# Splitting x earlier, halving the norm's maximum and lower parts, and one weight split per token tile

## The chip, the cores and the metric

The kernel runs on one core of one Trainium2 chip. The metric is the device time of one execution in microseconds. A core has TensorE (PE, matrix products into PSUM banks; PEld is its weight load), VectorE (DVE), ScalarE (ACT), GpSimd (POOL) and SyncE (SP, which issues the DMAs). Each engine works through its own row of instructions in order. An instruction whose operand isn't ready holds everything behind it in the row.

## The reference

Attention over 2 x 12 heads of 448 tokens with 64 columns, then two feed-forward networks on the 896 tokens, all in fp32:

```python
scores = cap * np.tanh(scale * (q @ k.T) / cap)
x = softmax(scores) @ v                 # heads side by side: 896 x 768
h = x @ w_in                            # 896 x 1024
e = np.exp(h - h.max(-1))
solu = h * e / (e.sum(-1) + 1e-9)
ln = (solu - solu.mean(-1)) / np.sqrt(solu.var(-1) + 1e-6) * g_ln
y = ln @ w_out                          # 896 x 768
p = sigmoid(y @ w_gate) * (y @ w_val)   # 896 x 1536
out = p @ moe2_w_out                    # 896 x 768
```

## The kernel before, in words

**Products in three passes.** An fp32 operand is split into an upper part, rounded to the multiplier's format (a cast on ACT), and a lower part, the rest (a subtraction on DVE or POOL). A product is then three matrix instructions: upper x upper, upper x lower, lower x upper. The weights arrive as 64-bit words and are turned to fp32 by bit operations on DVE (lines 320 to 323) before they are split.

**Stages.** Attention runs first, by pairs of heads. Two of the seven token tiles of the first network (128 tokens each, t = 0 and 1) are worked beside it, in slots of a table (`at`, `phase`). Tile 2 is begun at its end. The loop at line 584 does t = 2 to 6: first the 36 products of layer 1 for tile t (`l1_mms`, line 390), then `ln_trans(t - 1)`, eight transposes of the tile before, then the norm's chain of tile t. Layer 2 follows (line 620, the rows that write l2o and big from lnhi and lnlo): tokens 0 to 383 first, for each kk = 0 to 7 of the inner dimension six products (two rounds of kk = 0 to 3, then kk = 4 to 7 with all six), and after kk = 4 the transposes of tile 6. Then come tokens 384 to 895, then layer 3 (the gates) and layer 4.

**The norm's chain of a tile.** `ln_max` is a DVE maximum over the 1024 columns in PSUM (line 400). `ln_exp` is an exponential with its sum on ACT (405), into a tile e of which there is one. `ln_he` multiplies h and e on DVE (408). `ln_stats` takes two halves of statistics, their aggregate and a sum on DVE (415 to 419), and an inverse root on POOL (420). `ln_norm` takes a bias on DVE (424) and the scaled e on ACT (426, `late`). After the transposes, `ln_evac` casts the tile on ACT (440) and takes the lower part on DVE (441).

**What lies between.** `x_split(t)` makes the parts xh and xl of x that tile t's products read (377 and 378). There are two buffers of each, so tile t + 2 takes those of tile t. `w2_split(kk)` makes the two parts of w_out's slab kk, w_hi on ACT (515) and w_lo on DVE (512). They wait in the list `todo`, from which `fill(2)` takes the next slab's two steps. Before each kk, layer 2 calls `fill(1)` until that slab is there (lines 644 and 649).

**What sets the order.** Up to the end of layer 2, PE, ACT, DVE and POOL run in the order in which the code is written (`manual_schedule`, line 444). The weights of layer 3 (`load_slabs`, line 665: L315 and L337 on ACT, L320 to L323 and L340 on DVE) stand outside that order and are placed between by the scheduler. Two banks l2o serve layer 2; a later product takes a bank once the parts of y are taken from it (629 and 630).

Of the kernel before, what the change touches and what calls it, by code (L numbers as in the profile page):

```python
# [10 lines left out]
F32 = mybir.dt.float32  # L11
# [4 lines left out]
ALU = mybir.AluOpType  # L16
AX = mybir.AxisListType
# [3 lines left out]
P = 128  # L21
# [14 lines left out]
GROUPS = ((0, G1), (G1, NT))  # L36
# [11 lines left out]
L1_BESIDE = 2  # L48
# [20 lines left out]
def f32(ap):  # L69
    return ap.bitcast(F32)  # L70
# [7 lines left out]
def fused_kernel(ctx: ExitStack, tc: tile.TileContext, qk, v, cap, w_in, w_mid, g_ln, w_gv, w_fin, outT):  # L78
# [52 lines left out]
    with tc.If(bounded > 0) as cmp:  # L131
        network(tc, sh, False, w_in, w_mid, w_gv, w_fin, outT)
# [5 lines left out]
def network(ctx: ExitStack, tc: tile.TileContext, sh, general, w_in, w_mid, w_gv, w_fin, outT):  # L138
    nc = tc.nc
# [18 lines left out]
    lin2 = wi.enter_context(tc.tile_pool(name="lin2" + sfx, bufs=2, side="left"))  # L158
# [129 lines left out]
    def fill(k):  # L288
        for _ in range(min(k, len(todo))):
            todo.popleft()()  # L290
# [76 lines left out]
    hts, sts, lnes = {}, {}, {}  # L367

    def x_split(t, eng=nc.vector):
        xh = lin2.tile([P, K1, P], F32R, tag="xh", name="xh")  # L370
        xl = lin2.tile([P, K1, P], F32R, tag="xl", name="xl")
        t0 = t * P
        for b in range(B):
            lo, hi_ = max(t0, b * S), min(t0 + P, (b + 1) * S)
            if lo < hi_:
                src = x_sb[b][:, :, lo - b * S:hi_ - b * S]
                nc.scalar.copy(xh[:, :, lo - t0:hi_ - t0], src)  # L377
                eng.tensor_tensor(xl[:, :, lo - t0:hi_ - t0], src, f32(xh[:, :, lo - t0:hi_ - t0]), ALU.subtract)  # L378
        x_parts[t] = xh, xl

    def l1_mms(t):

        out = []

        def mm(half, kk, m):
            if t not in hts:
                hts[t] = big()
            xh, xl = x_parts[t]
            l, r = ((xh, wi_hi), (xh, wi_lo), (xl, wi_hi))[m]
            nc.tensor.matmul(hts[t][:, half], l[:, kk], r[:, half, kk], start=(kk == 0 and m == 0), stop=(kk == K1 - 1 and m == 2))  # L390

        for half in range(2):
            for kk in range(K1):
                for m in range(3):
                    out.append(lambda half=half, kk=kk, m=m: mm(half, kk, m))
        return out

    def ln_max(t):
        sts[t] = lin2.tile([P, 24], F32, tag="st", name="st")
        nc.vector.tensor_reduce(sts[t][:, 0:1], hts[t].rearrange("p a b -> p (a b)"), AX.X, ALU.max, negate=True)  # L400

    def ln_exp(t):
        st = sts[t]
        lnes[t] = lin2.tile([P, F1], F32, tag="e", name="e", bufs=1)
        nc.scalar.activation(lnes[t], hts[t].rearrange("p a b -> p (a b)"), AF.Exp, bias=st[:, 0:1], accum_out=st[:, 1:2])  # L405

    def ln_he(t):
        nc.vector.tensor_tensor(lnes[t], hts.pop(t).rearrange("p a b -> p (a b)"), lnes[t], ALU.mult)  # L408
# [21 lines left out]
    def ln_trans(t):  # L430
        e = lnes[t]
        lnes[t] = tp = big()
        for kk in range(K2):
            nc.tensor.transpose(tp[:, kk // 4, (kk % 4) * P:(kk % 4 + 1) * P], e[:, kk * P:(kk + 1) * P], ident)

    def ln_evac(t):
        g = 0 if t < 3 else 1
        c = slice(t * P - GROUPS[g][0], t * P - GROUPS[g][0] + P)
        tv = lnes.pop(t).rearrange("p a (k b) -> p (a k) b", b=P)
        nc.scalar.copy(ln_hi[g][:, :, c], tv)  # L440
        nc.vector.tensor_tensor(ln_lo[g][:, :, c], tv, f32(ln_hi[g][:, :, c]), ALU.subtract)  # L441


    order = nullcontext() if general else tc.manual_schedule(engines=ORDERED)
# [20 lines left out]
    def at(slot, phase, f, *a):  # L465
        beside.setdefault((slot, phase), []).append(lambda: f(*a))

    def run(fs):
        while fs:
            fs.pop(0)()  # L470
# [5 lines left out]
    for t in range(L1_BESIDE):  # L476
        s0 = S_L1 + L1_SLOTS * t
        s1 = s0 + L1_SLOTS
        at(s0, 2, x_split, t)
        for k in range(L1_SLOTS):  # L480
            at(s0 + 1 + k, 0 if k else 2, lambda t=t, k=k: run(l1_mms(t)[n_mm * k:n_mm * k + n_mm]))
        at(s1, 3, ln_max, t)
        at(s1 + 1, 1, ln_exp, t)
        at(s1 + 1, 2, ln_he, t)
        at(s1 + 1, 2, ln_stats, t)
        at(s1 + 1, 3, ln_norm, t)
        at(s1 + 3, 0, ln_trans, t)
        at(s1 + 3, 1, ln_evac, t)
        if t == L1_BESIDE - 1:
            at(s1, 2, x_split, t + 1)  # L490

# [15 lines left out]
    def w2_split(kk):  # L507
        g, w, hi = sh.g_sb[:, kk:kk + 1], f32(w2_w[kk]), w2_hi[:, kk]

        def lower():  # L510
            lo = w2a.tile([P, DM], F32R, tag="w", name="w2_lo")
            nc.vector.scalar_tensor_tensor(lo, w, g, f32(hi), ALU.mult, ALU.subtract)  # L512
            w2.append((hi, lo))

        return [lambda: nc.scalar.activation(hi, w, AF.Identity, scale=g), lower]
# [49 lines left out]
    t = L1_BESIDE  # L565
# [5 lines left out]
    late = []  # L571
# [12 lines left out]
    for t in range(L1_BESIDE, 7):  # L584
        if t == 2:
            x0.close()
            lnt2 = lns.enter_context(tc.tile_pool(name="lnt2" + sfx, bufs=1, side="right", reuse_waits="tile"))
            ln_hi[1] = lnt2.tile([P, K2, NT - G1], F32R, name="lnhi1")
            ln_lo[1] = lnt2.tile([P, K2, NT - G1], F32R, name="lnlo1")
            w2b = lns.enter_context(tc.tile_pool(name="w2b" + sfx, bufs=1, side="right", reuse_waits="tile"))  # L590
            w2_hi = w2b.tile([P, K2, DM], F32R, name="w2_hi")
            for kk in range(K2):
                todo.extend(w2_split(kk))
        mms = mms[24:] if t == L1_BESIDE else l1_mms(t)
        run(mms)
        if t > L1_BESIDE:
            ln_trans(t - 1)
        else:
            run(late[:1])
        ln_max(t)  # L600
        fill(2)
        ln_exp(t)
        ln_he(t)
        ln_stats(t)
        if t > L1_BESIDE:
            ln_evac(t - 1)
        else:
            run(late[1:])
        ln_norm(t, True)
        if t + 2 < 7:  # L610
            x_split(t + 2, nc.gpsimd)
            fill(2)
    wi.close()
    ytp = ctx.enter_context(tc.tile_pool(name="ytp" + sfx, bufs=1, side="left", reuse_waits="tile"))
    y_hi = ytp.tile([P, K3, NT], F32R, name="y_hi")
# [7 lines left out]
    def l2_mm(o, m, g, kk):  # L623
        w = [part[:, m * P:(m + 1) * P] for part in w2[kk]]
        prods(o, w, ln_hi[g][:, kk], ln_lo[g][:, kk], kk == 0, kk == K2 - 1)
# [14 lines left out]
    for ms in ((0, 1, 2, 3), (4, 5)):  # L640
        b = big()
# [6 lines left out]
    for kk in range(W2_EARLY, K2):  # L648
        while len(w2) <= kk:
            fill(1)  # L650
        for m in range(K3):
            l2_mm(accs[m], m, 0, kk)
        if kk == W2_EARLY:
            ln_trans(6)
            ln_evac(6)
    for m in range(K3):
        y_evac(accs[m], m, 0)
    for m in range(K3):
# [35 lines left out]
    for fc in range(K4):  # L694
# [4 lines left out]
        for z in range(2):  # L699
            o = big()  # L700
            for hf in range(2):
                for kk in range(K3):
                    c = slice(hf * HT, hf * HT + HT)
# [11 lines left out]
    for m in range(DM // P):  # L715
# [3 lines left out]
        for hf in range(2):  # L719
            c = slice(hf * HT, hf * HT + HT)  # L720
# [41 lines left out]
```

## Time and profile before

| | |
|---|---|
| median of 3 runs | 517.36 us (516.28 to 517.64) |
| profiled execution | 517.01 us, of which the span is 515.2 us |
| PE busy | 496.3 us, 96% of the span |
| DVE, ACT, POOL busy | 307.8, 235.6, 57.0 us |
| granted clock of TensorE | 1.00 |

The span runs from the profile's first instruction to its last. A busy PE is a modelled figure: its instructions are pipelined, so the start of one to the start of the next tells what it costs, and its duration is longer than that. A wait is written as the idle time before an instruction, with what ended it.

### The profile page before, as it was taken

What the parts mean: (1) busy time and instruction counts of PE and PEld (TensorE: products, weight loads), DVE (VectorE), ACT (ScalarE), POOL (GpSimd) and SP (SyncE); (2) the same over time, 40 slices, a digit from 0 to 9 for tenths busy, and PEclk for the clock granted to TensorE, in tenths of its full rate; (3) what the DMA queues carried; (4) which work ended last, traced back from release to release, by engine and by line L of the source; (5) the groups of instructions that cost most, each with busy time, mean ns of one, the idle gap of its engine ahead of it and who ended that gap; (6) DMA issues with size and microseconds to landing.
All of it is one profiled execution on the core that took longest, in us unless ns stands there. A gap on an engine that the chain in (4) does not pass through costs nothing.

```text
span 515.2 us, 6254 instructions
## 1 busy us (share of the span) xinstructions
PE 496.3 (96%) x2496; PEld 385.6 (75%) x2496; DVE 307.8 (60%) x416; ACT 235.6 (46%) x288; POOL 57.0 (11%) x41
## 2 busy tenths in 40 slices
PE   8999999998988889999999999999999999999995
PEld 5323323544566669988899999999999999999995
DVE  0778787556576686721488767767766675553000
ACT  4999999675325552410354333433233322232100
POOL 0010220103021210000010111111111011000000
PEclk9999999999999999999999999999999999999999
DMA  7757568633000003120045433333333323400001
GB/s 256 232 184 247 180 190 273 195 98 124 36 1 1 1 0 122 28 98 0 1 132 185 153 95 110 123 102 93 113 123 122 116 80 131 158 37 36 20 36 41
DMA packets 15313, 55.03 MB, mean 107 GB/s; under 512 B 2796, under 2 KB 5740, under 8 KB 15276
## 3 DMA queue, kind: packets, MB, share of 16 engines
q1 hardware_dynamic: 15276, 54.56, 33.2%
q8 instruction: 21, 0.34, 0.3%
q14 instruction: 16, 0.13, 0.1%
HBM read 51.68 MB, written 2.79 MB: 106 GB/s over the span
## 4 chain that ended last, share of the span: by engine, by line
PE 82%; ACT 8%; DVE 7%; issue 1%; POOL 1%; DMA 0%; ACTq 0%; POOLq 0%
PE big L620 37%; PE l4o L620 17%; PE l2o L620 8%; PE o L228 7%; PE big L188 6%; PE big L390 3%; PE sums L231 3%; ACT e L194 2%; ACT e L216 2%; DVE e L408 1%; DVE st L400 1%; DVE w_lo L512 1%; ACT e L405 1%; ACT e L426 1%; DVE lnlo L441 1%
## 5 line engine op out<-in xcount | busy, mean ns | idle before, releaser
L620 PE MATMUL big<-y_hi,w_hl 128*128 128x448 f32 x576 | 161.6, 362 | 0.0
L620 PEld LDWEIGHTS big<-y_hi,w_hl 128*128 128x128 f32 x576 | 107.9, 187 | 8.0
L620 PE MATMUL big<-y_lo,w_hl 128*128 128x448 f32 x288 | 104.6, 363 | 0.0
L620 PE MATMUL l4o<-p_hi,w_hl 128*128 128x448 f32 x288 | 80.6, 361 | 0.0
L337 ACT CAST w_hl<-w 128x768 fp32r<-128x768 f32 x36 | 29.8, 834 | 91.0 <-PE big L620 77.0
L620 PEld LDWEIGHTS l4o<-p_hi,w_hl 128*128 128x128 f32 x288 | 54.0, 187 | 4.1
L620 PEld LDWEIGHTS big<-y_lo,w_hl 128*128 128x128 f32 x288 | 54.1, 188 | 3.1
L340 DVE TENSOR_TENSOR w_hl<-w,w_hl 128x768 fp32r<-128x768 f32 x36 | 34.2, 954 | 32.9 <-ACT w_hl L337 32.9
L194 ACT ACTIVATE e<-big,cap_inv 112x896 f32<-112x896 f32 x48 | 46.1, 1021 | 16.1 <-PE big L188 16.1
L320 DVE TENSOR_SCALAR w<-w 128x768 f32<-128x768 f32 x44 | 37.8, 860 | 24.9 <-ACT w L315 24.3
L620 PE MATMUL l4o<-p_lo,w_hl 128*128 128x448 f32 x144 | 52.1, 363 | 0.0
L711 POOL TENSOR_TENSOR p_lo<-sg,p_hi 128x896 fp32r<-128x896 f32 x12 | 25.7, 2141 | 200.5 <-ACT p_hi L710 200.5
L216 ACT ACTIVATE e<-e,cap_abs 112x896 f32<-112x896 f32 x48 | 47.7, 1056 | 0.0
L188 PE MATMUL big<-qk_raw 64*112 64x448 f32 x192 | 44.4, 563 | 1.6 <-DVE st L414 1.3
L228 PE MATMUL o<-e,v 112*64 112x448 f32 x192 | 43.7, 552 | 1.9 <-issue 1.0
L323 DVE SCALAR_TENSOR_TENSOR w<-w_raw,w 128x768 uint32<-128x768 uint32 x44 | 43.9, 998 | 1.0
L322 DVE SCALAR_TENSOR_TENSOR w<-w_raw,w 128x768 uint32<-128x768 uint32 x44 | 43.7, 996 | 1.0
L315 ACT ACTIVATE w<-w_raw 128x768 f32<-128x768 f32 x36 | 32.3, 903 | 15.3 <-DVE w_hl L340 14.8
L188 PEld LDWEIGHTS big<-qk_raw 64*112 64x112 f32 x192 | 16.0, 174 | 28.7 <-issue 21.8
L390 PE MATMUL big<-wi_hi,xl 128*128 128x512 f32 x84 | 33.2, 396 | 3.3 <-POOL xl L378 3.3
L228 PEld LDWEIGHTS o<-e,v 112*64 112x64 f32 x192 | 14.1, 136 | 28.0 <-issue 14.9
L390 PE MATMUL big<-wi_hi,xh 128*128 128x512 f32 x84 | 34.1, 406 | 0.8 <-ACT xh L377 0.8
(95 smaller groups left out, 603.0 us busy)
## 6 DMA issues: line engine op xcount, KB each, us to landing
w_raw<-in_w_gv SPq DMA_DIRECT2D x24, 768.0 KB, 4.4
w_raw<-in_w_fin SPq DMA_DIRECT2D x12, 768.0 KB, 4.3
w_raw<-in_w_in SPq DMA_DIRECT2D x8, 768.0 KB, 5.9
w_raw<-in_w_mid SPq DMA_DIRECT2D x8, 768.0 KB, 5.5
qk_raw<-in_qk SPq DMA_DIRECT2D x12, 448.0 KB, 4.7
v<-in_v SPq DMA_DIRECT2D x12, 224.0 KB, 2.6
out_t<-ob SPq DMA_DIRECT2D x12, 224.0 KB, 1.9
qk_raw<-rd SPq DMA_DIRECT2D x22, 112.0 KB, 3.0
```

Of the source, the lines that this page charges most:

```text
L188: nc.tensor.matmul(sc[j][:KC, c, :S], r[d, 1, kc * KC:(kc + 1) * KC], r[d, 0], start=True, stop=True)
L194: nc.scalar.activation(e, es[n, u][:KC, :, :S], AF.Tanh, scale=sh.cap_inv[:KC])
L216: nc.scalar.activation(es[n, u], es[n, u], AF.Exp, scale=sh.cap_abs[:KC])
L228: nc.tensor.matmul(o[d, :S], vs[i][:, kc, d], e[j][:, c], start=(kc == 0), stop=(kc == 3))
L315: first = lambda t, lo, hi: nc.scalar.activation(f32(t), f32(hi), AF.Abs)
L320: word(lambda t, lo, hi: v.tensor_scalar(f32(t), f32(t), as_f32(W_MOST), as_f32(W_LEAST), ALU.min, ALU.max)),
L322: word(lambda t, lo, hi: v.scalar_tensor_tensor(t, hi, TOP, t, ALU.bitwise_and, ALU.bitwise_or)),
L323: word(lambda t, lo, hi: v.scalar_tensor_tensor(t, lo, 29, t, ALU.logical_shift_right, ALU.bitwise_or)),
L337: nc.scalar.copy(st["hi"], st["w"])
L340: nc.vector.tensor_tensor(st["lo"], st["w"], f32(st["hi"]), ALU.subtract)
L390: nc.tensor.matmul(hts[t][:, half], l[:, kk], r[:, half, kk], start=(kk == 0 and m == 0), stop=(kk == K1 - 1 and m == 2))
L620: nc.tensor.matmul(out, l, r, start=(first and m == 0), stop=(last and m == 2))
```

## The change

`ln_max` takes the two halves of the columns one after the other, each as soon as its half's products are done, and then the smaller of the two negated maxima. `ln_evac` makes the cast at its first call and the lower part of four of the eight blocks at each of two calls. In the loop `x_split(t + 2)` moves from the end of tile t to behind its maximum, and its lower part from POOL to DVE. The first lower half of tile t - 1 stays behind the statistics, the second comes behind the bias. There is one `fill(2)` at a tile's end instead of one behind the maximum and one at the end, so layer 2 finds five slabs of w_out split, not eight, and takes the other three in its own kk loop.

```diff
--- before.py
+++ after.py
@@ -395,9 +395,12 @@
                     out.append(lambda half=half, kk=kk, m=m: mm(half, kk, m))
         return out
 
-    def ln_max(t):
-        sts[t] = lin2.tile([P, 24], F32, tag="st", name="st")
-        nc.vector.tensor_reduce(sts[t][:, 0:1], hts[t].rearrange("p a b -> p (a b)"), AX.X, ALU.max, negate=True)
+    def ln_max(t, half):
+        if t not in sts:
+            sts[t] = lin2.tile([P, 24], F32, tag="st", name="st")
+        nc.vector.tensor_reduce(sts[t][:, 21 + half:22 + half], hts[t][:, half], AX.X, ALU.max, negate=True)
+        if half:
+            nc.vector.tensor_tensor(sts[t][:, 0:1], sts[t][:, 21:22], sts[t][:, 22:23], ALU.min)
 
     def ln_exp(t):
         st = sts[t]
@@ -433,12 +436,15 @@
         for kk in range(K2):
             nc.tensor.transpose(tp[:, kk // 4, (kk % 4) * P:(kk % 4 + 1) * P], e[:, kk * P:(kk + 1) * P], ident)
 
-    def ln_evac(t):
+    def ln_evac(t, half):
         g = 0 if t < 3 else 1
-        c = slice(t * P - GROUPS[g][0], t * P - GROUPS[g][0] + P)
-        tv = lnes.pop(t).rearrange("p a (k b) -> p (a k) b", b=P)
-        nc.scalar.copy(ln_hi[g][:, :, c], tv)
-        nc.vector.tensor_tensor(ln_lo[g][:, :, c], tv, f32(ln_hi[g][:, :, c]), ALU.subtract)
+        k, c = slice(half * 4, half * 4 + 4), slice(t * P - GROUPS[g][0], t * P - GROUPS[g][0] + P)
+        tv = lnes[t].rearrange("p a (k b) -> p (a k) b", b=P)
+        if half == 0:
+            nc.scalar.copy(ln_hi[g][:, :, c], tv)
+        else:
+            del lnes[t]
+        nc.vector.tensor_tensor(ln_lo[g][:, k, c], tv[:, k], f32(ln_hi[g][:, k, c]), ALU.subtract)
 
 
     order = nullcontext() if general else tc.manual_schedule(engines=ORDERED)
@@ -479,13 +485,15 @@
         at(s0, 2, x_split, t)
         for k in range(L1_SLOTS):
             at(s0 + 1 + k, 0 if k else 2, lambda t=t, k=k: run(l1_mms(t)[n_mm * k:n_mm * k + n_mm]))
-        at(s1, 3, ln_max, t)
+        at(s1, 3, ln_max, t, 0)
+        at(s1, 3, ln_max, t, 1)
         at(s1 + 1, 1, ln_exp, t)
         at(s1 + 1, 2, ln_he, t)
         at(s1 + 1, 2, ln_stats, t)
         at(s1 + 1, 3, ln_norm, t)
         at(s1 + 3, 0, ln_trans, t)
-        at(s1 + 3, 1, ln_evac, t)
+        at(s1 + 3, 1, ln_evac, t, 0)
+        at(s1 + 3, 1, ln_evac, t, 1)
         if t == L1_BESIDE - 1:
             at(s1, 2, x_split, t + 1)
 
@@ -597,19 +605,23 @@
             ln_trans(t - 1)
         else:
             run(late[:1])
-        ln_max(t)
-        fill(2)
+        ln_max(t, 0)
+        ln_max(t, 1)
+        if t + 2 < 7:
+            x_split(t + 2)
         ln_exp(t)
         ln_he(t)
         ln_stats(t)
         if t > L1_BESIDE:
-            ln_evac(t - 1)
-        else:
-            run(late[1:])
+            ln_evac(t - 1, 0)
+        else:
+            late[1]()
         ln_norm(t, True)
-        if t + 2 < 7:
-            x_split(t + 2, nc.gpsimd)
-            fill(2)
+        if t > L1_BESIDE:
+            ln_evac(t - 1, 1)
+        else:
+            late[2]()
+        fill(2)
     wi.close()
     ytp = ctx.enter_context(tc.tile_pool(name="ytp" + sfx, bufs=1, side="left", reuse_waits="tile"))
     y_hi = ytp.tile([P, K3, NT], F32R, name="y_hi")
@@ -652,7 +664,8 @@
             l2_mm(accs[m], m, 0, kk)
         if kk == W2_EARLY:
             ln_trans(6)
-            ln_evac(6)
+            ln_evac(6, 0)
+            ln_evac(6, 1)
     for m in range(K3):
         y_evac(accs[m], m, 0)
     for m in range(K3):
```

**ACT, from the scaled e of tile 2 to that of tile 3.** L426 (L429 in the changed kernel) is the scaled e, L377 the upper part of x, L515 (L523) w_hi of one slab, L405 (L408) the exponential, L440 (L444) the cast of the tile before. Before:

```order
L426 ACTIVATE e<-e,st 128x1024
L377 CAST xh<-x_159 128x768
L515 ACTIVATE w_hi<-w_w,g_sb 128x768 x2
L405 ACTIVATE e,st<-big,st 128x1024
L440 CAST lnhi_142<-big 128x8x128
L426 ACTIVATE e<-e,st 128x1024
```

and now:

```order
L429 ACTIVATE e<-e,st 128x1024
L523 ACTIVATE w_hi<-w_w,g_sb 128x768
L377 CAST xh<-x_159 128x768
L408 ACTIVATE e,st<-big,st 128x1024
L444 CAST lnhi_142<-big 128x8x128
L429 ACTIVATE e<-e,st 128x1024
```

The split of x stands behind one w_hi instead of in front of two.

**DVE, from the sum of a tile's statistics to the next tile's product of h and e.** L419 (L422) is the sum, L441 (L447) the lower part of the tile before, L424 (L427) the bias, L512 (L520) w_lo, L400 (L401, and L403 for the smaller of two) the maximum. Before:

```order
L419 TENSOR_TENSOR st<-st 128x1
L441 TENSOR_TENSOR lnlo_143<-big,lnhi_142 128x8x128
L424 TENSOR_SCALAR st<-st 128x1
L512 SCALAR_TENSOR_TENSOR w_lo<-w_w,g_sb,w_hi 128x768
L400 TENSOR_REDUCE st<-big 128x1
L512 SCALAR_TENSOR_TENSOR w_lo<-w_w,g_sb,w_hi 128x768
L408 TENSOR_TENSOR e<-big,e 128x1024
```

and now:

```order
L422 TENSOR_TENSOR st<-st 128x1
L447 TENSOR_TENSOR lnlo_143<-big,lnhi_142 128x4x128
L427 TENSOR_SCALAR st<-st 128x1
L447 TENSOR_TENSOR lnlo_143<-big,lnhi_142 128x4x128
L520 SCALAR_TENSOR_TENSOR w_lo<-w_w,g_sb,w_hi 128x768
L401 TENSOR_REDUCE st<-big 128x1 x2
L403 TENSOR_TENSOR st<-st 128x1
L378 TENSOR_TENSOR xl<-x_159,xh 128x768
L411 TENSOR_TENSOR e<-big,e 128x1024
```

One w_lo is gone, xl has come in behind the maximum, and half of the lower part has moved behind the bias.

**ACT, from the last tile's exponential to the weights of layer 3.** L337 is the upper part of layer 3's first weights. Before:

```order
L405 ACTIVATE e,st<-big,st 128x1024
L440 CAST lnhi_1200<-big 128x8x128
L426 ACTIVATE e<-e,st 128x1024
L440 CAST lnhi_1200<-big 128x8x128
L337 CAST w_hl<-w_1878 128x768
L337 CAST w_hl<-w_1889 128x768
```

and now:

```order
L408 ACTIVATE e,st<-big,st 128x1024
L444 CAST lnhi_1205<-big 128x8x128
L429 ACTIVATE e<-e,st 128x1024
L523 ACTIVATE w_hi<-w_w,g_sb 128x768
L444 CAST lnhi_1205<-big 128x8x128
L523 ACTIVATE w_hi<-w_w,g_sb 128x768 x3
L337 CAST w_hl<-w_1899 128x768
L337 CAST w_hl<-w_1910 128x768
```

Four w_hi stand here that stood earlier: one in front of the last tile's cast, three behind it.

**DVE, from the weights of layer 3 to the first lower part of y.** L340 is the lower part of layer 3's first weights, L320 to L323 the bit operations on its next, L630 (L642) the lower part of y. Before, beginning with the last tile's lower part:

```order
L441 TENSOR_TENSOR lnlo_1201<-big,lnhi_1200 128x8x128
L340 TENSOR_TENSOR w_hl<-w_1878,w_hl 128x768
L340 TENSOR_TENSOR w_hl<-w_1889,w_hl 128x768
L320 TENSOR_SCALAR w_1907<-w_1907 128x768
L321 TENSOR_SCALAR w_1907<-w_1907 128x768
L320 TENSOR_SCALAR w_1918<-w_1918 128x768
L322 SCALAR_TENSOR_TENSOR w_1907<-w_raw,w_1907 128x768
L321 TENSOR_SCALAR w_1918<-w_1918 128x768
L323 SCALAR_TENSOR_TENSOR w_1907<-w_raw,w_1907 128x768
L630 TENSOR_TENSOR y_lo<-l2o,y_hi 128x384
```

and now, beginning behind that lower part and two w_lo:

```order
L340 TENSOR_TENSOR w_hl<-w_1899,w_hl 128x768
L520 SCALAR_TENSOR_TENSOR w_lo<-w_w,g_sb,w_hi 128x768
L340 TENSOR_TENSOR w_hl<-w_1910,w_hl 128x768
L320 TENSOR_SCALAR w_1928<-w_1928 128x768
L321 TENSOR_SCALAR w_1928<-w_1928 128x768
L320 TENSOR_SCALAR w_1939<-w_1939 128x768
L322 SCALAR_TENSOR_TENSOR w_1928<-w_raw,w_1928 128x768
L321 TENSOR_SCALAR w_1939<-w_1939 128x768
L323 SCALAR_TENSOR_TENSOR w_1928<-w_raw,w_1928 128x768
L322 SCALAR_TENSOR_TENSOR w_1939<-w_raw,w_1939 128x768
L323 SCALAR_TENSOR_TENSOR w_1939<-w_raw,w_1939 128x768
L642 TENSOR_TENSOR y_lo<-l2o,y_hi 128x384 x2
```

A w_lo has come in, and both of the next weights' last steps stand ahead of y instead of one of them.

## Rows read from the trace of the kernel before

**Rows 1.** Two stretches, each engine's busy time, then granted clock.

```profile
148.00:192.00 44.00, 37.80 (x177) 29.70 (x177) 32.50 (x49) 21.91 (x28) 7.68 (x7) 1.00 0.00 1
...
192.00:510.00 318.00, 317.99 (x1592) 295.52 (x1590) 180.74 (x215) 98.94 (x125) 26.25 (x13) 1.00 0.28 90
```

**Rows 2.** TensorE in order of time: start, duration, instruction, wait before it.

```profile
179.26 1.09 PE L434 MATMUL big<-ident,e 128*128 128x128 f32 x8 [0.94 <-ACT e L426]
...
181.94 0.50 PE L390 MATMUL big<-wi_hi,xl 128*128 128x512 f32 x1 [1.11 <-POOL xl L378]
...
189.55 0.39 PE L390 MATMUL big<-wi_hi,xl 128*128 128x512 f32 x1
...
190.87 1.09 PE L434 MATMUL big<-ident,e 128*128 128x128 f32 x8 [0.94 <-ACT e L426]
...
191.72 0.43 PE L620 MATMUL l2o<-lnhi,w_hi 128*128 128x384 f32 x1
```

**Rows 3.** DVE in order of time, tile 4's end and tile 5's chain.

```profile
180.80 1.89 DVE L512 SCALAR_TENSOR_TENSOR w_lo<-w_w,g_sb,w_hi 128x768 fp32r<-128x768 f32 x1 [2.87 <-ACT w_hi L515]
...
182.62 1.21 DVE L400 TENSOR_REDUCE st<-big 128x1 f32<-128x1024 f32 x1
...
183.75 1.00 DVE L512 SCALAR_TENSOR_TENSOR w_lo<-w_w,g_sb,w_hi 128x768 fp32r<-128x768 f32 x1
...
185.18 1.23 DVE L408 TENSOR_TENSOR e<-big,e 128x1024 f32<-128x1024 f32 x1 [0.43 <-ACT e L405]
...
188.13 0.16 DVE L419 TENSOR_TENSOR st<-st 128x1 f32<-128x1 f32 x1
...
188.21 1.22 DVE L441 TENSOR_TENSOR lnlo<-big,lnhi 128x1024 fp32r<-128x1024 f32 x1
...
189.34 0.20 DVE L424 TENSOR_SCALAR st<-st 128x1 f32<-128x1 f32 x1
```

**Rows 4.** ACT in order of time, the same stretch.

```profile
177.97 1.24 ACT L426 ACTIVATE e<-e,st 128x1024 f32<-128x1024 f32 x1 [3.52 <-DVE st L424]
...
179.11 0.82 ACT L377 CAST xh<-x 128x768 fp32r<-128x768 f32 x1
...
179.84 1.76 ACT L515 ACTIVATE w_hi<-w_w,g_sb 128x768 fp32r<-128x768 f32 x2
...
183.95 1.12 ACT L405 ACTIVATE e<-big,st 128x1024 f32<-128x1024 f32 x1 [2.35 <-DVE st L400]
```

**Rows 5.** POOL in order of time, the same stretch.

```profile
180.06 1.82 POOL L378 TENSOR_TENSOR xl<-x,xh 128x768 fp32r<-128x768 f32 x1 [2.69 <-issue]
...
188.43 0.55 POOL L420 TENSOR_TENSOR st<-st,mhalf 128x1 f32<-128x1 f32 x1 [6.55 <-DVE st L419]
```

**Rows 6.** Chain that ended last, tile 0's norm: start, duration, what.

```profile
109.70 1.14 DVE st L400
...
110.86 1.21 ACT e L405 x2
...
116.50 1.74 PE big L188 x6
```

**Rows 7.** DVE groups by form: one instruction that reads 512 columns.

```profile
L630 DVE TENSOR_TENSOR y_lo<-l2o,y_hi 128x512 fp32r<-128x512 f32 x6 | 4.1, 692 | 27.0 <-ACT y_hi L629 27.0
```

**Rows 8.** DVE in order of time, the last tile's chain.

```profile
192.62 1.23 DVE L320 TENSOR_SCALAR w<-w 128x768 f32<-128x768 f32 x2
...
200.91 0.16 DVE L419 TENSOR_TENSOR st<-st 128x1 f32<-128x1 f32 x1
```

**Rows 9.** TensorE, the last tile's transposes and the second group's first product.

```profile
207.45 1.03 PE L434 MATMUL big<-ident,e 128*128 128x128 f32 x8
...
217.68 0.39 PE L620 MATMUL l2o<-lnhi,w_hi 128*128 128x512 f32 x1
```

**Rows 10.** ACT, the last tile's cast.

```profile
208.52 1.02 ACT L440 CAST lnhi<-big 128x1024 fp32r<-128x1024 f32 x1 [4.90 <-PE big L434]
```

**Rows 11.** DVE, the first lower part of y.

```profile
216.40 0.55 DVE L630 TENSOR_TENSOR y_lo<-l2o,y_hi 128x384 fp32r<-128x384 f32 x1
```

## The prediction, on record before the result

> **What bounds the kernel now.** I read the stretches first [rows 1]. From 192 to 510 us PE is busy for 317.99 of 318.00 us, so nothing there can be won except by starting it sooner. From 148 to 192 us, the loop over tiles 2 to 6, PE has 37.80 of 44.00 us: 6.2 us are idle. Then I read PE's own order [rows 2]. In each round it waits twice, 0.94 us in front of the transposes for the scaled e, and 1.11 us in front of a tile's third product for xl from POOL. The transposes of tiles 4 and 5 start at 179.26 and 190.87: the round takes 11.61 us. PE alone needs less. Transposes to the next product take 0.85 us (190.87 to 191.72), and 33 steps of a tile's products 7.61 (181.94 to 189.55), 0.23 each, so all 36 about 8.3: 9.2 us.
>
> What sets 11.61 is found by following the scaled e back through ACT and DVE [rows 3, 4]. It is a ring. Scaled e of tile 4 at 177.97; 1.14 to the split of x (179.11); 0.73 to w_hi (179.84); 0.96 to w_lo (180.80); 1.82 to the maximum (182.62); 1.33 to the exponential (183.95); 1.23 to h times e (185.18); 2.95 to the sum of the statistics (188.13); 0.08 to the lower part (188.21); 1.13 to the bias (189.34); 0.24 to the scaled e of tile 5 (189.58, by the 1.29 that lie between scaled e and transposes). The sum is 11.61. Both waits of PE hang on this ring, and DVE reaches the maximum of a tile whose products are long done only after a w_lo that waits for ACT.
>
> **The loop after the change.** The ring loses the cast of x (0.73), since w_hi now stands directly behind the scaled e. Its w_lo is the next question. The one at 180.80 takes 1.89 us and the one at 183.75 takes 1.00, and POOL's xl runs from 180.06 to 181.88, over the first [rows 3, 5]. With xl gone from POOL I price every w_lo at 1.00, 0.93 to the next start; the other end is 1.89.
>
> By the Trainium skill, "SBUF — State Buffer", section "Who interferes with whom", a DVE instruction with two SBUF inputs is held for the whole of a GpSimd instruction that reads SBUF and began first. The trace agrees: 181.88 plus most of 1.00 is where the long one ends (182.69). By that rule each w_lo would be short, and without it the rival with long ones below would be as likely as mine.
>
> No row shows a maximum over 512 columns. The nearest is a subtraction out of PSUM over 512 columns, 0.69 us [rows 7]; the whole maximum is the upper end, 1.21, and half of it, 0.61, the lower. I take 0.69: 0.61 to an independent next start (the whole one gives up 0.08 so), 0.72 to one that needs it. The smaller of two is a one-column instruction, 0.16 as the sum at 188.13, and 0.12 leads on to ACT, as behind the maximum. Where the lower part stood in front of the bias (0.08 + 1.13), POOL's root now ends last: 0.30 until it starts, 0.55, and 0.03 [rows 3, 5]. Half the lower part (0.69) fits beside that. The ring is then 1.14 + 0.96 + 0.93 + 0.61 + 0.72 + 0.28 + 1.23 + 2.95 + 0.30 + 0.58 + 0.24 = 9.94 us.
>
> That stays above PE's 9.2, so the wait for the scaled e remains at some 0.7 us. The wait for xl goes: the split of tile t + 2 now runs a whole round before its products. ACT's part (0.82) runs beside the maxima, DVE's (at most 1.00, as w_lo of the same size) beside the exponential's 1.23. It costs nothing while it is shorter than that cover, and 0.3 a round if it took 1.5. The first half of the maximum is ready early but stands behind w_lo in DVE's row, so it wins no start.
>
> Three rounds (transposes of tile 2 to those of tile 5) win 3 x 1.67 = 5.0 us. Against that, tile 0's maximum stands on the chain of waits [rows 6]: maximum, exponential, PE. It grows from 1.14 to 0.61 + 0.72 + 0.16 = 1.49, that is +0.35. Tile 1's lies ahead of DVE's wait for the last pair's sums and I take it at nothing, at most the same 0.35. Tile 2's maximum stands behind the split of tile 3 in both kernels: its halves add 0.28 and the earlier bias takes 0.33 back. So tile 2 is 0.3 late, the loop wins 4.7, and layer 2 starts at 187.0 instead of 191.72.
>
> **What layer 2 gives back.** Before, all eight slabs were split when layer 2 began. Now slab 4 is split behind the last tile's scaled e, and slabs 5 to 7 behind its cast, on ACT's row.
>
> Slab 4: the scaled e of tile 5 starts at 184.9 (190.87 - 4.7 - 1.29), its w_lo at 187.0, the halves of tile 6's maximum at 187.9, and layer 3's first bit operation behind them at 189.1. From that instruction to the sum of tile 6's statistics took 8.29 us [rows 8], with the same instructions between as now and the one-column minimum (0.1) added: 197.5. Root, bias and 0.24 put the scaled e of tile 6 at 198.6, w_hi at 199.8 to 200.7, and w_lo ends at 201.8. PE would be at kk = 4 after 72 of the 90 products that took 15.73 us (191.72 to 207.45 [rows 2, 9]), 0.175 each: at 199.6, and at its third product, the first to need w_lo, at 199.95. It loses 1.8 us.
>
> Slabs 5 to 7: PE starts tile 6's transposes at 199.6 + 18 x 0.175 + 1.8 = 204.55. Their cast begins 1.07 later (207.45 to 208.52 [rows 9, 10]), 205.6, and ends 1.02 later. Behind it come w_hi of slab 5 (until 207.5) and, on DVE, two lower halves (206.7 to 207.9) and w_lo, done at 208.9. PE would want that w_lo at 204.55 + 0.85 + 0.35 = 205.75. It loses 3.2 us. Slabs 6 and 7 follow at about 0.9 us each on either engine, PE needs 3.15 us a slab: no loss.
>
> So far 517.01 - 4.7 + 1.8 + 3.2 = 517.3, with PE at the second token group at 218.0 (217.68 + 0.3). That group's first product needs a bank l2o, so the first lower part of y. From the last tile's cast to it DVE took 7.88 us (208.52 to 216.40 [rows 10, 11]). It now has three w_lo more in between (2.8) and two more steps on layer 3's weights (about 1.8, as two w_lo): 205.6 + 12.5 = 218.1, ending at 218.65. Another 0.7 us. The rest of PE's row is as before, without a wait [rows 1], and moves as one.
>
> **Sum.** 517.01 - 4.7 + 1.8 + 3.2 + 0.7 = 518.0 us. The sum stands on the profiled execution, 517.01; the median of the three runs is 0.35 above it and their spread 1.4, so I leave it at 518.0. About 1.55 us (0.3%) is what a measurement of this kernel can tell from no change. The forecast is thus 4.7 us won in the loop and 5.7 given back in layer 2. Its own range follows from halves at 0.61 instead of 0.69 (ring, tiles 0 and 2, lower parts: about -0.8) or 0.85 (+1.5), and 0.1 for each of five new restarts of PE: 517.0 to 519.6.
>
> **Rivals.** *The gain stays.* Layer 2 doesn't wait, and 517.0 - 4.7 = 512.3. For it speaks that PE waits nowhere from 192 us on and that ACT is busy for only 98.94 of those 318 us [rows 1]. Against it, the splits stand in ACT's row behind instructions that themselves wait for tile 6, and an engine with idle time can't pass them. Slab 4 would have to come 1.8 us and slab 5 3.2 us earlier than worked out.
>
> *PE sets the round.* If the links of the ring overlap more than before's did, the round falls to PE's 9.2. For it speaks that the first half of the maximum is ready long before it is read; against it, that each link of the ring waits for the one before. Layer 2 starts 3 x 0.74 = 2.2 us sooner, tile 6's chain too, and the losses in layer 2 stay: 515.8.
>
> *The long w_lo stays (slower).* If 1.89 us comes from something other than POOL, say from the w_hi of the next slab that ran beside it, a round is 10.8 us. Four w_lo lie ahead of layer 2 (+3.6), those of slabs 4 and 5 delay PE by 0.9 each, and the two behind them hold y: 518.0 + 3.6 + 1.8 + 0.6 = 524.0. From an average of some 1.2 us a w_lo the kernel would be slower beyond doubt. For it speaks that the long one stands right behind ACT's pair of w_hi [rows 3, 4]; against it, that the short one at 183.75 has ACT work beside it as well, the exponential at 183.95.
>
> **Chances.** Forecast 0.70, of which 0.52 falls within 0.3%, 0.16 above and 0.02 below. The gain stays 0.13, faster. PE sets the round 0.11, half of it within and half faster. Long w_lo 0.06, slower. That makes faster 0.20, same 0.58, slower 0.22. The range 515.6 to 519.8 leaves out the first and the last rival, 0.19, and takes in the forecast's bounds and the second.
>
> **What would show it.** In the changed profile the transposes of tiles 3, 4 and 5 stand 9.9 us apart, with a wait of about 0.7 us for the scaled e and none for xl. Every w_lo takes about 1.0 us. Layer 2 starts near 187 us. At kk = 4 PE waits some 1.1 us for w_hi and 0.7 for w_lo, at kk = 5 about 2 for w_hi and 1 for w_lo, and 0.7 for y at the second group, which starts near 218.7 us. I am wrong if layer 2 starts at 187 and those waits aren't there, or if the rounds differ from 9.9 by more than 0.4.

## The result, and the profile after

The change made the kernel slower: 521.39 us (521.19 to 521.89) against 517.38 (516.28 to 517.64) on the same chip, a ratio of 1.0083 (95% interval 1.0066 to 1.0101). The forecast of 518.0 and its range up to 519.8 were both too low. The profiled execution took 521.89 us, span 520.1 for 515.2 before.

First the loop and layer 2: TensorE of the changed kernel in order of time (start, duration, instruction, and in brackets the wait before it). L437 are the transposes of tiles 2 to 6, L632 the products of layer 2.

```profile
159.30 1.09 PE L437 MATMUL big<-ident,e 128*128 128x128 f32 x8
...
169.27 1.09 PE L437 MATMUL big<-ident,e 128*128 128x128 f32 x8 [0.66 <-ACT e L429]
...
179.21 1.09 PE L437 MATMUL big<-ident,e 128*128 128x128 f32 x8 [0.66 <-ACT e L429]
...
189.16 1.09 PE L437 MATMUL big<-ident,e 128*128 128x128 f32 x8 [0.64 <-ACT e L429]
190.01 0.43 PE L632 MATMUL l2o<-lnhi,w_hi 128*128 128x384 f32 x1
...
203.64 0.44 PE L632 MATMUL l2o<-lnhi,w_hi 128*128 128x384 f32 x1 [0.86 <-ACT w_hi L523]
...
204.69 0.44 PE L632 MATMUL l2o<-lnhi,w_lo 128*128 128x384 f32 x1 [0.43 <-DVE w_lo L520]
...
207.58 1.03 PE L437 MATMUL big<-ident,e 128*128 128x128 f32 x8
210.55 0.44 PE L632 MATMUL l2o<-lnhi,w_hi 128*128 128x384 f32 x1 [1.94 <-ACT w_hi L523]
...
211.97 0.44 PE L632 MATMUL l2o<-lnhi,w_lo 128*128 128x384 f32 x1 [0.80 <-DVE w_lo L520]
...
214.60 0.52 PE L632 MATMUL big<-lnhi,w_hi 128*128 128x384 f32 x1
214.92 0.52 PE L632 MATMUL big<-lnlo,w_hi 128*128 128x384 f32 x1
...
222.69 0.39 PE L632 MATMUL l2o<-lnhi,w_hi 128*128 128x512 f32 x1
```

The rounds are 9.95 us (179.21 to 189.16) where they were 11.61 [rows 2]; the wait for xl is gone. Yet layer 2 starts only 1.7 us sooner, at 190.01, since the loop itself starts 3.2 us later (below). Layer 2 waits where it was said to. In the end the second token group starts at 222.69, 5.0 us later than before [rows 9]. At 214.60 two products lie 0.32 us apart, and those at 204.97 to 207.4 lie 0.175 apart.

DVE of the changed kernel in the same order: w_lo, the maximum's halves, the smaller of the two, and the bias.

```profile
180.02 1.02 DVE L520 SCALAR_TENSOR_TENSOR w_lo<-w_w,g_sb,w_hi 128x768 fp32r<-128x768 f32 x1 [1.54 <-ACT w_hi L523]
180.95 1.28 DVE L401 TENSOR_REDUCE st<-big 128x1 f32<-128x512 f32 x2
182.27 0.16 DVE L403 TENSOR_TENSOR st<-st 128x1 f32<-128x1 f32 x1
...
187.61 0.21 DVE L427 TENSOR_SCALAR st<-st 128x1 f32<-128x1 f32 x1
```

w_lo takes 1.02 us for the 1.89 of [rows 3], and two halves take 1.28 for 1.21 in one piece.

Now the stretch in front of the loop, where pairs of heads run beside tile 0. TensorE of before, then of after, and behind it tile 0's h times e on DVE in the changed kernel. L188 are scores, which start when that h times e has ended (the brackets name DVE's next instruction); L390 are tile 1's products, L228 the next attention products.

```profile
116.48 1.75 PE L188 MATMUL big<-qk_raw 64*112 64x448 f32 x6 [1.26 <-DVE st L414]
...
118.74 0.39 PE L390 MATMUL big<-wi_hi,xl 128*128 128x512 f32 x1
...
121.11 1.35 PE L228 MATMUL o<-e,v 112*64 112x448 f32 x6
...
156.08 1.09 PE L434 MATMUL big<-ident,e 128*128 128x128 f32 x8
```

```profile
116.64 2.71 PE L188 MATMUL big<-qk_raw 64*112 64x448 f32 x6 [1.53 <-DVE st L417]
...
120.30 0.63 PE L390 MATMUL big<-wi_hi,xl 128*128 128x512 f32 x1
...
124.47 1.72 PE L228 MATMUL o<-e,v 112*64 112x448 f32 x8
```

```profile
115.37 1.22 DVE L411 TENSOR_TENSOR e<-big,e 128x1024 f32<-128x1024 f32 x1
```

The scores start 0.16 us later, but from them to the attention products it is 7.83 us instead of 4.63, with the same instructions between. The reason stands in the stretches of the changed kernel (busy time of PE, PEld, DVE, ACT, POOL, then TensorE's granted clock):

```profile
116.00:118.00 2.00, 1.36 (x5) 0.75 (x6) 2.00 (x5) 0.09 (x1) 0.00 (x0) 0.83 0.03 8
118.00:120.00 2.00, 2.00 (x4) 0.62 (x3) 1.26 (x5) 1.53 (x2) 1.10 (x2) 0.50 0.00 0
...
122.00:124.00 2.00, 2.00 (x6) 1.61 (x5) 1.97 (x2) 0.25 (x1) 1.48 (x1) 0.50 0.82 338
...
212.00:214.00 2.00, 2.00 (x9) 1.99 (x10) 1.99 (x3) 1.67 (x4) 0.00 (x0) 0.72 0.00 0
214.00:216.00 2.00, 2.00 (x8) 2.00 (x7) 2.00 (x3) 1.14 (x2) 0.00 (x0) 0.50 0.00 0
216.00:218.00 2.00, 2.00 (x12) 2.00 (x11) 1.97 (x4) 0.67 (x1) 0.00 (x0) 0.93 0.00 0
```

In two places TensorE runs at half its clock, 1.2 GHz for 2.4: behind the wait in front of the scores, 1.53 us for 1.26, and behind the two new waits at kk = 5. The page's row of the clock shows the same two dents and no other:

```profile
PEclk9999999997999999899999999999999999999999
```

A longer wait of the same execution has no fall behind it. In front of attention products at 74 us TensorE waits 1.83 us (0.85 before, in code that the change doesn't touch), and the stretch behind it is at full clock. So the length of a wait alone doesn't decide it.

```profile
74.02 1.72 PE L228 MATMUL o<-e,v 112*64 112x448 f32 x8 [1.83 <-ACT e L194]
```

```profile
74.00:76.00 2.00, 1.98 (x12) 0.72 (x16) 1.97 (x5) 2.00 (x4) 0.00 (x0) 1.00 0.02 4
```

The busy share hides a half clock. PE is 100% busy in 118 to 124 us, only with longer instructions: busy time alone would tell of good use.

The account from before to after, by the starts shown: tile 0's scores +0.16; half clock behind them 3.20, of which 3.06 are left at tile 2's transposes (159.30 against 156.08, +3.22 in all); three rounds -4.93 (29.86 for 34.79); kk = 4 of layer 2 +1.84 (190.01 to 207.58 is 17.57 for 15.73); from the last transposes to the second group +4.88 (15.11 for 10.23). Of the last, 3.19 are the two waits of kk = 5 (210.55 less 207.58 + 0.85, and 211.97 less 210.55 + 0.35), and 1.69 are left for the half clock: the three stretches give 0.28 x 2 + 0.50 x 2 + 0.07 x 2 = 1.70. The sum is +5.0, and the spans differ by 4.9.

### The profile page after: what moved, and what is told of

It is laid out like the page before. It is cut to its first block, busy times and chain, and to the rows that moved or that the text cites. A ratio compares the mean times of both kernels' runs of the same rounds, so it can differ in the third digit from the quotient of the medians.

```text
span 520.1 us, 6272 instructions
## 1 busy us (share of the span) xinstructions
PE 500.3 (96%) x2496; PEld 388.9 (75%) x2496; DVE 311.0 (60%) x440; ACT 235.8 (45%) x288; POOL 50.3 (10%) x38
## 4 chain that ended last, share of the span: by engine, by line
PE 78%; ACT 10%; DVE 8%; issue 2%; POOL 1%; POOLq 0%; ACTq 0%
PE big L632 35%; PE l4o L632 17%; PE l2o L632 7%; PE o L228 5%; PE big L188 5%; PE big L390 5%; ACT e L194 3%; ACT e L216 3%; PE sums L231 3%; DVE e L411 1%; DVE w_lo L520 1%; DVE st L401 1%; ACT e L429 1%; ACT w_hi L523 1%; PE warm L120 1%
## 5 line engine op out<-in xcount | busy, mean ns | idle before, releaser
L632 PE MATMUL big<-y_hi,w_hl 128*128 128x448 f32 x576 | 161.9, 362 | 0.0
L632 PEld LDWEIGHTS big<-y_hi,w_hl 128*128 128x128 f32 x576 | 107.9, 187 | 8.2
L632 PE MATMUL big<-y_lo,w_hl 128*128 128x448 f32 x288 | 104.6, 363 | 0.0
L632 PE MATMUL l4o<-p_hi,w_hl 128*128 128x448 f32 x288 | 80.7, 361 | 0.0
L337 ACT CAST w_hl<-w 128x768 fp32r<-128x768 f32 x36 | 29.8, 833 | 91.9 <-PE big L632 77.8
L632 PEld LDWEIGHTS l4o<-p_hi,w_hl 128*128 128x128 f32 x288 | 54.0, 187 | 3.9
L632 PEld LDWEIGHTS big<-y_lo,w_hl 128*128 128x128 f32 x288 | 54.1, 188 | 2.9
L340 DVE TENSOR_TENSOR w_hl<-w,w_hl 128x768 fp32r<-128x768 f32 x36 | 34.3, 954 | 33.0 <-ACT w_hl L337 32.9
L320 DVE TENSOR_SCALAR w<-w 128x768 f32<-128x768 f32 x44 | 37.6, 857 | 24.6 <-ACT w L315 24.2
L632 PE MATMUL l4o<-p_lo,w_hl 128*128 128x448 f32 x144 | 52.1, 363 | 0.0
L188 PE MATMUL big<-qk_raw 64*112 64x448 f32 x192 | 45.0, 566 | 1.9 <-DVE st L417 1.5
L228 PE MATMUL o<-e,v 112*64 112x448 f32 x192 | 43.5, 552 | 2.9 <-ACT e L194 1.8
L323 DVE SCALAR_TENSOR_TENSOR w<-w_raw,w 128x768 uint32<-128x768 uint32 x44 | 43.8, 997 | 1.0
L188 PEld LDWEIGHTS big<-qk_raw 64*112 64x112 f32 x192 | 15.9, 173 | 28.8 <-issue 22.4
L390 PE MATMUL big<-wi_hi,xh 128*128 128x512 f32 x84 | 35.2, 418 | 0.8 <-ACT xh L377 0.8
L228 PEld LDWEIGHTS o<-e,v 112*64 112x64 f32 x192 | 14.4, 136 | 28.5 <-issue 16.5
L390 PE MATMUL big<-wi_lo,xh 128*128 128x512 f32 x84 | 33.7, 401 | 0.0
```

Source lines behind the costliest of these rows:

```text
L188: nc.tensor.matmul(sc[j][:KC, c, :S], r[d, 1, kc * KC:(kc + 1) * KC], r[d, 0], start=True, stop=True)
L228: nc.tensor.matmul(o[d, :S], vs[i][:, kc, d], e[j][:, c], start=(kc == 0), stop=(kc == 3))
L320: word(lambda t, lo, hi: v.tensor_scalar(f32(t), f32(t), as_f32(W_MOST), as_f32(W_LEAST), ALU.min, ALU.max)),
L323: word(lambda t, lo, hi: v.scalar_tensor_tensor(t, lo, 29, t, ALU.logical_shift_right, ALU.bitwise_or)),
L337: nc.scalar.copy(st["hi"], st["w"])
L340: nc.vector.tensor_tensor(st["lo"], st["w"], f32(st["hi"]), ALU.subtract)
```

## The experiments

My theory: the waits and the ring came as worked out, and TensorE's clock, which the forecast had left at full, costs the rest, because TensorE now waits longer in front of tile 0's scores and anew in layer 2. Rivals: the halves or the moved splits slow TensorE by themselves; or the lost time is the added instructions. Ratios are to the kernel before, run on the same chip.

**1. The changed kernel, tiles 0 and 1 with one maximum.**

```diff
-        at(s1, 3, ln_max, t, 0)
-        at(s1, 3, ln_max, t, 1)
+        at(s1, 3, ln_max_whole, t)
```

> The changed kernel with the maximum of tiles 0 and 1, the two beside attention, taken whole again. Theory: the half clock that TensorE shows from about 117.6 to 124 us followed from PE's wait of 1.53 us there (1.26 before), which the halves of tile 0's maximum lengthened. Then the wait is 1.26 again, the clock stays at 1.00 in that stretch, and the time is 521.4 - 3.4 = 518.0 us. Rival: the clock falls there for a reason that the halves don't touch; then only the length of the halves goes, 0.3 us, and the time is 521.1.

Measured: 518.72 us, ratio 1.0028 (1.0017 to 1.0040). Its TensorE, then its stretches:

```profile
115.98 1.75 PE L188 MATMUL big<-qk_raw 64*112 64x448 f32 x6 [1.26 <-DVE st L421]
...
206.73 0.44 PE L635 MATMUL l2o<-lnhi,w_hi 128*128 128x384 f32 x1 [1.94 <-ACT w_hi L526]
...
208.15 0.69 PE L635 MATMUL l2o<-lnhi,w_lo 128*128 128x384 f32 x1 [0.80 <-DVE w_lo L523]
```

```profile
118.00:120.00 2.00, 2.00 (x10) 1.63 (x9) 1.52 (x3) 2.00 (x4) 1.65 (x2) 1.00 0.00 0
...
209.00:211.00 2.00, 2.00 (x8) 2.00 (x7) 2.00 (x4) 1.67 (x3) 0.00 (x0) 0.50 0.00 0
```

With the wait back at 1.26 the first fall is gone, and the time is 2.7 us shorter than the changed kernel's on another chip. The second fall, behind layer 2's waits, stays and is longer in this profile: 0.50 in all three stretches from 208 to 214 us.

**2. The kernel before, with halves for tiles 0 and 1 alone.**

```diff
-        at(s1, 3, ln_max, t)
+        at(s1, 3, ln_max_half, t, 0)
+        at(s1, 3, ln_max_half, t, 1)
```

> The kernel before with nothing changed but the maximum of tiles 0 and 1 taken in halves. Theory as above: the wait grows past that of before, the clock falls to half for some 6 us, and the time is 517.4 + 0.3 + 3.1 = 520.8 us. Rival: the halves cost only their length, 517.7.

Measured: 518.39 us (515.79 to 520.00), ratio 1.0016 (0.9997 to 1.0035): neither value, but a mixture. Four of ten runs took 519.6 to 520.0 at a mean clock of 0.991 to 0.994, some 1 us short of the theory's value; the rest lie between 515.8 and 518.7, three of them at 0.994 too. The profiled run is one with the fall, behind the same 1.53 us:

```profile
117.71 1.75 PE L188 MATMUL big<-qk_raw 64*112 64x448 f32 x6 [1.53 <-DVE st L421]
```

```profile
120.00:122.00 2.00, 2.00 (x6) 1.61 (x5) 1.76 (x4) 2.00 (x3) 1.65 (x2) 0.50 0.00 0
```

So behind the wait in this place the clock falls in some executions and not in others. Where it falls the price differs too: from the scores to the attention products it is 6.19 us here (117.71 to 123.90) and 7.83 in the changed kernel's profile, for 4.63 at full clock.

**3. and 4. Two weight splits a round again, off the ring.** The second split of slabs is put where ACT and DVE wait for the root; in the fourth kernel together with the edit of the first.

```diff
+        if t < 5:
+            fill(1)
         ln_norm(t, True)
...
+        if t < 5:
+            fill(1)
         fill(2)
```

> The changed kernel with a second split of w_out for tiles 2 to 4, its ACT step between the cast and the scaled e, its DVE step behind the second lower half, so that all eight slabs are split before layer 2 needs them. Theory: layer 2's waits at kk = 4 and 5 and the half clock behind them cost 6.7 us together (layer 2 starts 1.7 us before that of the kernel before, its second group 5.0 after it) and go: 514.7 us, rounds of the loop still 9.9. Rival: the added steps lengthen the ring by the length of a split, 1.8 us a round for three rounds, 520.1.

> The changed kernel with both edits: the maximum of tiles 0 and 1 whole, and the second split off the ring. Theory: both gains add, 521.4 - 3.4 - 6.7 = 511.3 us, the clock at 1.00 throughout. Rival, if the half clock beside attention comes without the halves: 514.4.

Measured: 512.88 (ratio 0.9926, 0.9905 to 0.9946) and 511.48 (0.9879, 0.9858 to 0.9899). Layer 2 waits nowhere and its clock stays at 1.00 in both; the third kernel's profile still has the fall in front of attention:

```profile
118.00:120.00 2.00, 2.00 (x5) 1.61 (x6) 1.38 (x3) 2.00 (x4) 1.62 (x2) 0.50 0.00 0
...
190.00:220.00 30.00, 30.00 (x169) 28.91 (x168) 22.25 (x39) 11.70 (x17) 0.55 (x1) 1.00 0.32 106
```

The third kernel is 8.5 us faster than the changed one, on another chip (8.1 by the two ratios), where 6.7 had been expected: 5.0 for the late splits' waits and 1.7 for the clock behind them. The rest isn't theirs alone, since that comparison also holds executions in which the first fall was shorter or absent; in the profiles the scores come to the attention products in 6.22 us for 7.83. Between the fourth kernel and the first, on one chip, it is 7.2.

**5. The third kernel, halves kept, tile 0's h times e ahead of the weights' bit operations on DVE.**

```diff
-        at(s1 + 1, 2, ln_he, t)
+        at(s1 + 1, 1 if t == 0 else 2, ln_he, t)
```

> The run with the second split off the ring, maxima of tiles 0 and 1 still in halves, and tile 0's product of h and e put in front of the weights' bit operations in DVE's row, so that it no longer waits for ACT's abs of a weight chunk and the scores' bank comes free some 2.5 us earlier. Theory: the wait of 1.53 us goes, with it the half clock, though the halves stay: 512.9 - 1.5 - 1.1 = 510.3 us and clock 1.00. Rival: the halves bring the half clock; then 511.4 with the clock still falling.

Measured: 509.04 us, ratio 0.9845 (0.9810 to 0.9879). DVE now has h times e at 110.94, in the changed kernel at 115.37, and TensorE doesn't wait there:

```profile
110.94 1.22 DVE L411 TENSOR_TENSOR e<-big,e 128x1024 f32<-128x1024 f32 x1 [1.27 <-ACT e L408]
```

```profile
112.81 1.76 PE L188 MATMUL big<-qk_raw 64*112 64x448 f32 x8
```

```profile
118.00:120.00 2.00, 2.00 (x18) 0.33 (x14) 1.97 (x2) 0.90 (x2) 2.00 (x2) 1.00 0.54 111
```

The halves are still there, the clock is 1.00. So it is the wait and not the halves: all four runs have a mean clock of 0.997 to 0.999, where the third kernel's ten have 0.993 to 0.999.

**6. and 7. The kernel before, with the wait lengthened by two and by eight one-column minima.**

```diff
+    def ln_late(t):
+        st = sts[t]
+        for k in range(4):
+            nc.vector.tensor_tensor(st[:, 21:22], st[:, 0:1], st[:, 0:1], ALU.min)
+            nc.vector.tensor_tensor(st[:, 0:1], st[:, 21:22], st[:, 21:22], ALU.min)
...
         at(s1, 3, ln_max, t)
+        if t == 0:
+            at(s1, 3, ln_late, t)
```

> The kernel before, its maxima whole, with two one-column DVE minima between tile 0's maximum and its exponential (they change no value), so that PE's wait in front of the scores grows from 1.26 by about 0.45 to 1.7 us without any halved reduction. Theory: it is the length of that wait that lets TensorE's clock fall; then the clock is at half for some us behind it and the time is 517.1 + 0.45 + 1 to 3 = 518.6 to 520.6 us. Rival: the half clock belongs to the halved reductions themselves; then the clock stays at 1.00 and the time is 517.6.

> The kernel before with eight added one-column minima of 0.2 us on VectorE ahead of tile 0's exponential (they change no value): TensorE waits there about 1.26 + 1.65 = 2.9 us instead of 1.26, with whole maxima as before. My theory, that the length of the wait in front of attention is what lets TensorE's clock fall to half for some microseconds: the granted clock drops to about 0.5 behind the wait in nearly every run, and the time is the kernel before's of its batch (516.8) + 1.65 + 1.5 to 3, 520 to 521.5 us. Rival, that a wait costs its length only and the fall needs the halves or the moved splits: 518.5 us, clock 1.00 throughout.

Measured with two (the loop's body once): 517.87, ratio 1.0023 (1.0006 to 1.0040), a miss. The profiled run has a wait of 1.67 us and a clock of 1.00 throughout; seven of ten runs have a mean clock of 0.994, and they took 517.8 to 518.5. With eight: 520.91 (520.18 to 521.49), ratio 1.0080 (1.0063 to 1.0097), 3.8 us over the kernel before and so 2.2 more than the 1.55 by which the wait grew.

```profile
118.21 2.01 PE L188 MATMUL big<-qk_raw 64*112 64x448 f32 x6 [2.81 <-DVE st L420]
```

```profile
118.00:120.00 2.00, 1.79 (x6) 0.62 (x6) 1.93 (x7) 0.73 (x1) 0.00 (x0) 0.89 0.03 8
120.00:122.00 2.00, 2.00 (x5) 1.49 (x5) 1.33 (x4) 2.00 (x3) 1.53 (x2) 0.50 0.00 0
```

This kernel has nothing of the change in it. In front of the scores a wait of 2.8 us costs its length and half a clock behind it; all four runs have a mean clock of 0.991 to 0.994. With 1.5 to 1.7 us there it comes out one way or the other, and what decides stays open.

**8. The fourth kernel with whole maxima in the loop too.**

```diff
-        ln_max(t, 0)
-        ln_max(t, 1)
+        ln_max_whole(t)
```

> The run with both edits (maxima of tiles 0 and 1 whole, second split off the ring), and the maxima of tiles 2 to 6 whole as well. Theory: the first half never starts before its tile's last product, because DVE reaches it only behind w_lo, so the halves are 0.28 us longer a round (0.61 + 0.72 + 0.28 against 1.33) and buy nothing: rounds 9.66 instead of 9.94, 511.5 - 1.1 = 510.4 us. Rival: the early half hides half of the maximum, and the whole one costs about 0.5 us a round: 513.

Measured: 510.74 us, ratio 0.9875 (0.9841 to 0.9909). In the profile a round is 9.69 us, with a wait of 0.40 instead of 0.66:

```profile
174.94 1.09 PE L441 MATMUL big<-ident,e 128*128 128x128 f32 x8 [0.41 <-ACT e L433]
...
184.63 1.09 PE L441 MATMUL big<-ident,e 128*128 128x128 f32 x8 [0.40 <-ACT e L433]
```

Halving the maximum wins nothing and costs 0.26 a round. The medians of this kernel and the fourth, 0.7 apart, were taken on two chips, and their ratios are the same within the intervals: the profile shows the gain, the times don't.

**9. The kernel before, with the split of x alone moved to behind the maximum and to DVE.**

```diff
         ln_max(t)
+        if t + 2 < 7:
+            x_split(t + 2)
         fill(2)
...
-            x_split(t + 2, nc.gpsimd)
```

> The kernel before with one part of the change alone: the split of x goes ahead of both weight steps and its lower half from GpSimd to VectorE; two weight splits a round and the maximum in one instruction stay. My theory: the ring loses the cast of x (0.73) and the long w_lo's extra 0.89, but 1.80 us of VectorE work ahead of he outlast the exponential by about 0.4, so rounds of about 10.4 us for 11.61, no wait in layer 2 and the clock at 1.00 in front of attention: 513.5 us. Rival, that the rounds' gain came from the halves or from the single split: rounds of 11.3 or more, 516 to 517 us.

Measured: 513.73 us, ratio 0.9927 (0.9900 to 0.9955). Transposes, and what lies between the maximum and h times e on DVE:

```profile
167.16 1.09 PE L434 MATMUL big<-ident,e 128*128 128x128 f32 x8 [1.07 <-ACT e L426]
...
177.51 1.09 PE L434 MATMUL big<-ident,e 128*128 128x128 f32 x8 [1.06 <-ACT e L426]
```

```profile
168.90 1.22 DVE L400 TENSOR_REDUCE st<-big 128x1 f32<-128x1024 f32 x1
170.03 0.95 DVE L378 TENSOR_TENSOR xl<-x,xh 128x768 fp32r<-128x768 f32 x1
170.90 1.01 DVE L512 SCALAR_TENSOR_TENSOR w_lo<-w_w,g_sb,w_hi 128x768 fp32r<-128x768 f32 x1
171.83 1.21 DVE L408 TENSOR_TENSOR e<-big,e 128x1024 f32<-128x1024 f32 x1
```

This one part is 3.4 us faster than before, with rounds of 10.35. The second w_lo stands ahead of h times e, which starts 1.60 us behind the exponential (170.23 to 171.83), where the changed kernel has 1.24 (182.54 to 183.78). That is most of the 0.4 by which these rounds are longer than the changed kernel's, 1.2 in three rounds; what the single split saved so, layer 2 gave back as 5.0 us of waits.

**10. What the runs point to:** whole maxima, h times e of tiles 0 and 1 early, both splits of a tile off the ring (w_hi ahead of the scaled e, w_lo behind the second half of the lower part).

```diff
+        pairs = [todo.popleft() for _ in range(4 if t < 5 else 2)]
+        run(pairs[::2])
         ln_norm(t, True)
...
-        fill(2)
+        run(pairs[1::2])
```

> All together: maxima whole, h times e early for tiles 0 and 1, and both splits of a tile off the ring (their ACT steps in front of the scaled e, their DVE steps behind the second lower half). Theory: the ring falls to 9.1 us, below PE's 9.2, so PE sets the round and the waits for the scaled e go: 511.5 - 2.1 for the rounds - 1.3 for tile 0's wait - about 1 for tile 1's chain = 507.1 us. Rival: DVE's row, now with two w_lo in front of the maximum, takes the ring's place: rounds stay near 9.9 and the time is 509.2.

Measured: 505.47 us (504.66 to 505.77), ratio 0.9764 (0.9731 to 0.9797), faster than both and 1.6 below what was expected. The early h times e starts the loop 3.4 us sooner than experiment 8's on the same chip (tile 2's transposes at 152.24 for 155.66), where 2.3 had been worked out; what else is in the difference isn't shown. The loop's stretch, and all of TensorE's waits from 100 to 225 us (us in total, times, longest):

```profile
150.00:190.00 40.00, 40.00 (x206) 34.55 (x205) 36.52 (x63) 21.66 (x26) 2.73 (x5) 1.00 0.03 6
```

```profile
PE big L441 <- ACT e L194: 1.2, 1, 1.2
PE big L390 <- ACT xh L377: 0.4, 1, 0.4
```

TensorE has no wait left in the loop and its clock is 1.00 in every stretch of it.

## Why the prediction was wrong

**The loop: right.** The round was to be 9.94 and is 9.95, the wait 0.7 and is 0.64 to 0.66, w_lo 1.00 (0.93 to the next start) and is 1.02 (0.93); three rounds were to win 5.0 and win 4.93. From the maximum's first half to the exponential it is 1.59 (180.95 to ACT's start at 182.54) for 0.61 + 0.72 + 0.28. The long w_lo went with POOL's xl: from 150 to 205 us the kernels with xl on POOL (before, experiments 2, 6 and 7) have some of 1.84 to 1.90, and those with xl on DVE none above 1.07. Experiment 9 shows that the moved split of x carries most of the win, and experiment 8 that the halved maximum carries none. The halved lower part was not tried alone; in the traces it brings the bias from 1.21 to 0.88 us behind the sum's start (188.13 to 189.34 before, 186.73 to 187.61 after), the 0.33 that was worked out.

**Layer 2's waits: right.** kk = 4 was to lose 1.8 and loses 1.84, kk = 5 3.2 and loses 3.19. The third, 0.7 us for y at the second group, isn't there. DVE's row was priced rightly: from the last tile's cast to the first lower part of y it took 12.59 us (208.65 to 221.24) for 12.5. But TensorE came 1.7 us later than worked out because of its clock and found y ready. At full clock it would have been there at about 221.0, some 0.8 before that lower part's end (an estimate from these starts; no run shows it).

**The failed step: "It grows from 1.14 to 0.61 + 0.72 + 0.16 = 1.49, that is +0.35", so "tile 2 is 0.3 late".** The 1.49 is right (109.52 to 111.01 in the changed kernel), and the delay of the scores is even smaller than 0.35, 0.16. But the sum took a wait for its length and put the clock behind it at nothing. This one went from 1.26 to 1.53, TensorE fell to half its clock behind it, and tile 2 was 3.2 us late. Experiments 1, 5 and 7 show that the wait does it, without the halves as well; the wait of 1.83 us at 74 us shows that not every one does. The same error stands in layer 2 at another 1.7: "PE would be at kk = 4 after 72 of the 90 products ... 0.175 each" and so on count every product behind a wait at full clock. There the fall goes with the waits (experiments 3 and 4) and stays with them (experiment 1), but no run has those waits without the moved splits. With 2.9 at tile 0 (the 3.22 less the 0.3 that was counted) and 1.7 here, less the 0.7 for y, the forecast of 518.0 becomes 521.9, the profiled execution's 521.89.

The range was wrong for the same reason. Its bounds allowed "0.1 for each of five new restarts of PE"; no rival was a slower TensorE. Before's clock of 1.00 [rows 1] was taken as a property of the kernel, where it was one of the profiled execution: other executions of the same kernel have a lower mean clock (last section).

The profile of before would not have given the price, since it has no fall. But the Trainium skill, "TensorE: Matmul & The Clock Gate", section "A second HAM failure mode: psum-queue depth-cycling", tells of a kernel whose short and frequent idle times between groups of matmuls let the clock swing between half and full. The trace agrees in so far as the clock fell to 0.50 behind 1.53 us, though here it was a single wait and not many. A slower TensorE behind the waits should have been a rival with a chance of its own.

## What to carry to other kernels

A new or longer wait of TensorE is priced at its length and, as a rival, at a half clock behind it, which cost 1.6 to 3.2 us in front of attention here and 1.7 in layer 2; the granted clock by stretches shows it, the busy share doesn't. Where a shorter chain moves preparation behind it, ask in which stage that preparation now ends last: taking the second weight split off the round won part of 5 us and cost over 5 in layer 2, while putting it into a gap of the same chain won both. A change of several parts is worth taking apart: one part here is worth 3.4 us alone, another nothing, and a third, the single weight split, turned the sum.

## What the runs showed of the hardware that had not been expected

TensorE's granted clock fell to 0.50 behind single waits of 1.53 us in three profiles (the changed kernel and experiments 2 and 3), stayed at 1.00 behind 1.67 us in one (experiment 6) and behind 1.26 in the five profiles that have it, and fell behind 2.81 (experiment 7). All these waits stand in front of the same scores. At another place, in front of attention products at 74 us, it stayed at 1.00 behind 1.83 us in the changed kernel, 1.80 in experiments 4 and 10 and 1.71 in experiment 2. So the length of the wait alone doesn't tell whether the clock falls; what else does isn't shown. The same program had it in some executions and not in others: of the kernel before, in 45 runs beside the experiments, 8 had a mean clock of 0.994 and took 517.67 to 519.07 us, the others 514.91 to 518.45 at 0.997 to 1.000. Where in those runs the clock fell isn't known, since they left no trace. The mean counts the end of an execution too: experiment 5's profile, at 0.997, is below 1.00 only from 502 us on, where TensorE has nothing left to do.
